# A convolution, SoLU and projection kernel: tiles in threes instead of pairs, with PSUM as three pairs of banks and two single ones

## The chip, the cores and the metric

One core of a Trainium2 chip. The metric is the device time of one launch in microseconds. Before the change it was 1185.45 us, the median of three runs (1185.33 to 1186.61).

The engines are called PE (matmuls; PEld is its loading of weights), DVE, ACT (ScalarE), POOL and SP (which here only issues DMAs).

## The reference

Two stages, of which the second takes the first's output as its rows:

```python
# conv: x is 8 x 4160 x 192, weight 8 x 7; causal, softmax over the 7 taps, one filter for each group of 24 columns
out = np.einsum('hk,bskhg->bshg', w, x_unf)
# mlp: 33280 rows of 192, w_in 192 x 1024, w_out 1024 x 192
h = x @ w_in
e = np.exp(h - np.max(h, axis=-1, keepdims=True))
solu = h * (e / (np.sum(e, axis=-1, keepdims=True) + 1e-09))
mu = np.mean(solu, axis=-1, keepdims=True)
var = np.mean((solu - mu) ** 2, axis=-1, keepdims=True)
out = ((solu - mu) / np.sqrt(var + 1e-06) * g_ln) @ w_out
```

## The kernel before, in words

The 33280 rows are 260 tiles of 128. They come out of 17 chunks of the sequence: two short ones at the start of the first batch, then fifteen of 2080 rows (half a batch, some 16 tiles). Everything is written out by hand, in the order in which each engine runs it; nothing is reordered afterwards.

Nearly all matmuls (the first three chunks' convolutions run in float32) work on float16 halves: a float32 value is kept as an upper float16 and the remainder as a lower one, and a product is the sum of three.

**Convolution of a chunk.** x is loaded (L150), its largest magnitude is taken on DVE (`sum_squares`, L171, eight of them for a chunk) and a scale worked out, then it is split into two halves on POOL (L226, L230, L233). Eight groups of matmuls with a band matrix (L271) make the convolution; each group lies in one PSUM bank, from which ACT takes the upper half (`upper`, L303) and DVE the lower one (`lower`, L312). DMA transposes (`turn`, L342) bring the result into `yT`, where the 192 columns, in halves, are three blocks of 128 partitions: two full upper/lower blocks, and one that holds the last 64 columns' upper half on 64 partitions and the lower half on the other 64. `double` (L355) copies 64 rows of `yT` to the other 64 partitions, as `y2`.

**A tile.** The first product (`emit_rows`, L727) is eight matmuls of 128 x 512 into a pair of banks, `ph`. What is left is the product of the last 64 columns with the lower half of the weights, which has only 64 rows: the *thirds* (`emit_third`, L752), two matmuls for a tile. Of one tile of a pair they run on the upper 64 rows of the array (from `yT`), of the other on the lower 64 (from `y2`), side by side. From `ph`:

- DVE scales it and takes the row's minimum (`emit_max`, L773), since the sign is turned;
- ACT takes the exponential and its sum into `e` (`emit_exp`, L780);
- DVE multiplies the two into `e` and sums (`numerators`, L790); with that `ph` is free;
- ACT casts the product to float16, `p` (L798), and sums its squares (L802);
- POOL makes the remainder (`emit_lo`, L807), and a DMA transpose on SP's queue (L809) turns both halves into `pT`;
- PE makes the second product from `pT`, 16 matmuls into one bank, `po` (`emit_out`, L824), five tiles later;
- DVE adds the two halves of `po` (`emit_evac`, L831), and every eight tiles POOL works out the factors of the rows (L878 to L888), which are applied on POOL or DVE (L893, L897) and stored (L906).

**PSUM** has eight banks: `ps_h` two pairs for `ph`, `ps_c` two single ones for convolutions and sums, `ps_o` two for `po`.

**The order.** The first six tiles have functions of their own (`first_two`, `second_two`, `third_two`), in which the weights are scaled too; from tile 6 on `two_steps` takes two tiles at a time. On PE: the first tile's eight matmuls, the four thirds of both tiles, the second tile's eight, then second products of two earlier tiles and up to two groups of the convolution of a later chunk. `chores` says by fractions of a chunk which group, turn, load and maximum falls to which tile. `tail` finishes the last five tiles; their second products have four banks, since `po` of every other one is put in `ps_c`.

## Time and profile before

| | |
|---|---|
| median of three runs | 1185.45 us |
| the profiled execution | 1186.39 us |
| its span, first to last instruction | 1184.6 us |
| mean granted clock of PE | 0.992 |
| PE busy | 1148.0 us (97%) |
| DVE busy | 1036.0 us (87%) |
| POOL busy | 961.1 us (81%) |
| ACT busy | 952.7 us (80%) |
| DMA queue q1, share of 16 engines | 97.9% |

The profile is of one execution, 0.9 us over the median. The clock is 1.00 almost throughout; two stretches of some 7 us, from 29.3 and 73.6 us, have 0.50 and 0.51. In a row of the timeline the first number is the start, the second how long the instruction or group lasted; "x4" is a group of four, and the brackets at the end tell how long the engine had been idle and what it waited for. Matmuls overlap by their pipeline, so what one costs is read from the start of one to the start of the next.

### The profile page before, as it was taken

The numbers are of one execution on the slowest core, as the hardware profiler recorded it, in microseconds if no ns is written. First come the engines' busy times: TensorE is split into PE (matmuls) and PEld (weight loads), VectorE is DVE, ScalarE is ACT, GpSimd is POOL, SyncE is SP. The second block draws the span as 40 slices with busy tenths as digits, with TensorE's granted clock in tenths as the row PEclk, the third lists the DMA queues.
The fourth block names the chain that finished last, engine by engine and source line by source line (L and its number), as shares of the span: only waits on it lengthen the run. The fifth ranks groups of instructions, "written<-read, shape, count | busy, mean of one in ns | idle before, by whom it ended". The sixth has DMA issues, their size and how long they took to land.

```text
span 1184.6 us, 22276 instructions
## 1 busy us (share of the span) xinstructions
PE 1148.0 (97%) x7678; PEld 676.9 (57%) x7678; DVE 1036.0 (87%) x2081; ACT 952.7 (80%) x1525; POOL 961.1 (81%) x951
## 2 busy tenths in 40 slices
PE   5989999999999999999999999999999999999997
PEld 3455555556565565656555565655655555565555
DVE  7889899998988989899899988999898898787785
ACT  6968888788888787888877788887878878888883
POOL 1726989998979699797978979898897979867675
PEclk9889999999999999999999999999999999999999
DMA  8789799999999999999999999999999998989986
GB/s 234 151 173 179 158 220 198 203 198 204 204 194 205 194 205 185 214 203 201 203 174 197 188 215 214 187 204 175 215 196 198 208 193 156 171 171 179 191 152 155
DMA packets 727295, 226.95 MB, mean 192 GB/s; under 512 B 651518, under 2 KB 725774, under 8 KB 727182
## 3 DMA queue, kind: packets, MB, share of 16 engines
q1 hardware_dynamic: 727182, 225.53, 97.9%
q8 instruction: 60, 0.98, 0.3%
q14 instruction: 53, 0.43, 0.1%
HBM read 33.00 MB, written 25.56 MB: 49 GB/s over the span
## 4 chain that ended last, share of the span: by engine, by line
PE 63%; POOL 13%; issue 8%; DVE 7%; ACT 4%; DMA 1%; POOLq 0%; ACTq 0%; DVEq 0%
PE po L824 28%; PE ph L727 26%; POOL p L807 8%; PE pc L271 4%; PE ph L752 4%; DVE e L790 2%; DVE ph L773 2%; ACT e L780 1%; ACT p L798 1%; DMA pT<-p 1%; POOL raw L893 1%; POOL t L887 1%; DVE cvm L337 1%; DVE xa L171 1%; POOL xs L226 1%
## 5 line engine op out<-in xcount | busy, mean ns | idle before, releaser
L807 POOL TENSOR_TENSOR p<-e,p 128x1024 f16<-128x1024 f32 x259 | 551.2, 2138 | 153.5 <-ACT p L798 153.3
L824 PE MATMUL po<-ohl,pT 128*128 128x384 f16 (+1 forms) x4200 | 548.6, 285 | 3.2 <-DVE raw L831 2.6
L824 PEld LDWEIGHTS <-pT 128*128 128x128 f16 x4200 | 382.0, 98 | 152.4 <-issue 4.3
L727 PE MATMUL ph<-whi,yT 128*128 128x512 f16 x1548 | 422.8, 382 | 15.2 <-DVE e L790 15.1
L780 ACT ACTIVATE e<-ph,sm 128x1024 f32<-128x1024 f32 x260 | 289.7, 1114 | 160.6 <-DVE ph L773 145.2
L773 DVE TENSOR_SCALAR_CACHE_REDUCE ph<-ph,cv 128x1024 f32<-128x1024 f32 x248 | 317.8, 1290 | 99.3 <-PE ph L752 56.6
L727 PEld LDWEIGHTS <-yT 128*128 128x128 f16 x2064 | 189.5, 98 | 265.9 <-issue 58.4
L790 DVE SCALAR_TENSOR_TENSOR e<-ph,cv,e 128x1024 f32<-128x1024 f32 x248 | 317.0, 1278 | 8.4 <-ACT e L780 5.6
L798 ACT CAST p<-e 128x1024 f16<-128x1024 f32 x260 | 270.6, 1041 | 38.5 <-DVE e L790 33.0
L802 ACT ACTIVATE sq<-e 128x1024 f32<-128x1024 f32 x260 | 274.5, 1056 | 4.0
L727 PE MATMUL ph<-wlo,yT 128*128 128x512 f16 x516 | 154.7, 382 | 0.0
L831 DVE TENSOR_REDUCE raw<-po 128x192 f32<-128x384 f32 x255 | 140.7, 552 | 0.0
L233 POOL TENSOR_TENSOR xs<-xr,xs 128x960 f16<-128x960 f32 (+1 forms) x56 | 107.7, 1924 | 2.3
L752 PE MATMUL ph<-wlo,yT 64*128 64x512 f16 x268 | 81.5, 384 | 0.0
L312 DVE SCALAR_TENSOR_TENSOR y<-pc,y 112x432 f16<-112x432 f32 (+5 forms) x140 | 72.4, 534 | 5.4 <-ACT y L303 5.2
L752 PE MATMUL ph<-wlo,y 64*128 64x512 f16 x252 | 76.3, 383 | 0.0
L271 PE MATMUL pc<-xs,taps_hi 128*112 128x240 f16 (+1 forms) x448 | 73.0, 261 | 0.3 <-ACT taps_hi L569 0.3
L171 DVE TENSOR_REDUCE xa<-xr 128x1 f32<-128x384 f32 x120 | 69.3, 618 | 0.0
L303 ACT ACTIVATE y<-pc 112x432 f16<-112x432 f32 (+5 forms) x140 | 63.1, 472 | 0.1
L230 POOL TENSOR_SCALAR xr<-xr,s 128x960 f32<-128x960 f32 (+1 forms) x56 | 57.7, 1030 | 2.4
L271 PE MATMUL pc<-xs,taps_lo 128*112 128x240 f16 (+1 forms) x224 | 58.5, 261 | 0.0
L887 POOL TENSOR_TENSOR t<-t,mhalf 128x8 f32<-128x8 f32 (+2 forms) x33 | 53.7, 1626 | 2.6
(146 smaller groups left out, 772.4 us busy)
## 6 DMA issues: line engine op xcount, KB each, us to landing
out_dram<-raw SPq DMA_DIRECT2D x127, 192.0 KB, 2.6
xr<-in_x_dram SPq DMA_DIRECT2D x41, 480.0 KB, 4.6
xr<-in_x_dram SPq DMA_DIRECT2D x22, 384.0 KB, 4.2
pT<-p SPq DMA_TRANSPOSE x260, 4.6
y<-yT SPq DMA_DIRECT2D x15, 140.0 KB, 2.5
y<-yT SPq DMA_DIRECT2D x15, 126.0 KB, 2.4
yT<-y SPq DMA_TRANSPOSE x102, 3.6
raw_out<-in_moe_w_out_dram SPq DMA_DIRECT2D x1, 1536.0 KB
```

The costliest lines, as they stand in the source:

```text
L233: (2.1 * size + 0.2, lambda: pool.tensor_tensor(xl, r, h, ALU.subtract)),
L271: nc.tensor.matmul(o, tp[:, h + j, :], r, start=q == 0, stop=q == len(ops) - 1)
L727: nc.tensor.matmul(bank, lhs, w[:, r, n * 512 : (n + 1) * 512], start=start and j == 0, stop=stop and j == len(ops) - 1,)
L752: nc.tensor.matmul(banks_of(t)[n], y[q, t.off : t.off + P], wlo[q, 1, n * 512 : (n + 1) * 512], start=start, stop=not start,)
L773: dve.tensor_scalar(t.ph, t.ph, t.cv[:, 0:1], None, ALU.mult, ALU.min, accum_out=t.bias)
L780: act.activation(t.e, t.ph, AF.Exp, bias=t.bias, scale=-1.0, accum_out=grp.z[:, g : g + 1])
L790: dve.scalar_tensor_tensor(t.e, t.ph, t.cv[:, 3:4], t.e, ALU.mult, ALU.mult, accum_out=t.grp.s1[:, t.g : t.g + 1],)
L798: act.copy(t.p16[:, :, 0, :], t.halves)
L802: act.activation(junk, t.e, AF.Square, accum_out=t.grp.s2[:, t.g : t.g + 1])
L807: eng.tensor_tensor(t.p16[:, :, 1, :], t.halves, t.p16[:, :, 0, :], ALU.subtract)
L824: nc.tensor.matmul(t.po[:, 0:n], t.pT[:, a, :], w, start=j == 0, stop=j == len(ops) - 1)
L831: dve.tensor_reduce(t.grp.raw[:, t.g, :], t.po[:, 0 : 2 * D].rearrange("p (a d) -> p d a", a=2), AX.X, ALU.add,)
```

## The change

PSUM is one pool of three pairs of banks (`pair(0)` to `pair(2)`) and two single banks that take turns (`single`): `po`, convolutions, sums of a column and small products all draw from these two, in the order of the program. From tile 8 on, `three_steps` takes three tiles a, b, c with the pairs 0, 1, 2. `emit_a` makes a's eight matmuls and then the thirds of all three in one place: a's beside b's, two at a time, then c's own two side by side, the first on the upper rows from `yT`, the second on the lower rows from `y2`. b's eight matmuls follow. The second products of three earlier tiles stand ahead of a's matmuls, between b's and c's, and after c's. Convolution groups stand at up to four places: after the first second product, after b's matmuls, after the second, and after the last second product.

The tiles 0 to 7 keep their pairs (`fourth_two` is new); the convolutions of chunk 1 are held there in the third pair (`hold`), and the thirds of both tiles, all on the upper rows, stand in two places as before. The maxima and loads of a triple (`others`) are written at its head, ahead of L831 of the first second product. The sum of squares of c is taken in the next triple. The load of `g_ln` moves from the end of the first loads to behind the first transposes and a load of chunk 1. In `tail`, the second products use the two single banks, and the factor of the first of the five tiles is worked out there, not three tiles earlier.

PE at the thirds of tiles 56 and 57 (`ph_56`, `ph_57` are the tiles' pairs of banks, `yT_4` and `y2_4` chunk 4's convolution), before:

```order
L727 MATMUL ph_56_3293<-whi_111,yT_4_2330 128x512
L752 LDWEIGHTS yT_4_2330
L752 MATMUL ph_56_3293<-wlo_112,yT_4_2330 128x512
L752 LDWEIGHTS y2_4_2331
L752 MATMUL ph_57_3302<-wlo_112,y2_4_2331 128x512
...
L727 LDWEIGHTS yT_4_2330
L727 MATMUL ph_57_3302<-whi_111,yT_4_2330 128x512
```

and with the change, with tile 58 as the third:

```order
L733 MATMUL ph_56_3311<-whi_104,yT_4_2317 128x512
L758 LDWEIGHTS yT_4_2317
L758 MATMUL ph_56_3311<-wlo_105,yT_4_2317 128x512
L758 LDWEIGHTS y2_4_2318
L758 MATMUL ph_57_3320<-wlo_105,y2_4_2318 128x512
...
L758 MATMUL ph_58_3321<-wlo_105,yT_4_2317 128x512
L758 LDWEIGHTS y2_4_2318
L758 MATMUL ph_58_3321<-wlo_105,y2_4_2318 128x512
L733 LDWEIGHTS yT_4_2317
L733 MATMUL ph_57_3320<-whi_104,yT_4_2317 128x512
```

What is left out repeats the four rows for the other bank. Six thirds stand in one place, where four stood; over the whole program the places fall from 134 to 92.

DVE over the same tiles (`sm` is a row's minimum, `po` a second product, `y16` the lower half of a convolution, `raw` the output), before:

```order
L773 TENSOR_SCALAR ph_56_3293,sm_56_3358<-ph_56_3293,cv_4_1443 128x1024
L773 TENSOR_SCALAR ph_57_3302,sm_57_3362<-ph_57_3302,cv_4_1443 128x1024
L790 SCALAR_TENSOR_TENSOR e_56_3360,s1_56_3289<-ph_56_3293,cv_4_1443,e_56_3360 128x1024
L831 TENSOR_REDUCE raw_48_3166<-po_51_3317 128x192
L790 SCALAR_TENSOR_TENSOR e_57_3364,s1_56_3289<-ph_57_3302,cv_4_1443,e_57_3364 128x1024
L312 SCALAR_TENSOR_TENSOR y16_5_10_3277<-pc_5_10_2_3334,y16_5_10_3277 112x9x48
L897 TENSOR_SCALAR raw_40_2744,t1_40_2445<-raw_40_2744,t2_40_2446 128x192
L831 TENSOR_REDUCE raw_48_3166<-po_52_3341 128x192
```

and with the change:

```order
L845 TENSOR_REDUCE raw_48_3173<-po_51_3287 128x192
L322 SCALAR_TENSOR_TENSOR y16_5_10_3219<-pc_5_10_2_3304,y16_5_10_3219 112x9x48
L911 TENSOR_SCALAR raw_32_2307,t1_32_1995<-raw_32_2307,t2_32_1996 128x192
L788 TENSOR_SCALAR ph_56_3311,sm_56_3343<-ph_56_3311,cv_4_1328 128x1024
L788 TENSOR_SCALAR ph_57_3320,sm_57_3347<-ph_57_3320,cv_4_1328 128x1024
L805 SCALAR_TENSOR_TENSOR e_56_3345,s1_56_3276<-ph_56_3311,cv_4_1328,e_56_3345 128x1024
L845 TENSOR_REDUCE raw_48_3173<-po_52_3358 128x192
L805 SCALAR_TENSOR_TENSOR e_57_3349,s1_56_3276<-ph_57_3320,cv_4_1328,e_57_3349 128x1024
L788 TENSOR_SCALAR ph_58_3321,sm_58_3410<-ph_58_3321,cv_4_1328 128x1024
L845 TENSOR_REDUCE raw_48_3173<-po_53_3393 128x192
L805 SCALAR_TENSOR_TENSOR e_58_3412,s1_56_3276<-ph_58_3321,cv_4_1328,e_58_3412 128x1024
```

The first two tiles of a triple stand as a pair did, minimum, minimum, product, evacuation, product. The third follows by itself: minimum, evacuation, product, with nothing else between them.

The diff, cut to its core:

```diff
-    ps_h = ctx.enter_context(tc.tile_pool(name="ps_h", bufs=2, space=PSUM))
-    ps_c = ctx.enter_context(tc.tile_pool(name="ps_c", bufs=2, space=PSUM))
-    ps_o = ctx.enter_context(tc.tile_pool(name="ps_o", bufs=2, space=PSUM))
+    ps = ctx.enter_context(tc.tile_pool(name="ps", bufs=1, space=PSUM))
...
+    def pair(slot, name):
+        return ps.tile([P, F], F32, name=name, tag=f"pair{slot}")
+    singles = 0
+    def single(name):
+        nonlocal singles
+        singles += 1
+        return ps.tile([P, 512], F32, name=name, tag=f"single{singles % 2}")
...
+    def emit_a(a, b, c):
+        a.ph = pair(0, f"ph_{a.i}")
+        emit_rows(a, True, False)
+        b.ph, c.ph = pair(1, f"ph_{b.i}"), pair(2, f"ph_{c.i}")
+        for t, n, low in (
+            (a, 0, False), (b, 0, True), (a, 1, False), (b, 1, True),
+            (c, 0, False), (c, 1, True),
+        ):
+            emit_third(t, n, low, t is not a)
...
     def emit_out(t):
-        ps, tag = (ps_c, "cv") if t.last and t.i % 2 else (ps_o, "po")
-        t.po = ps.tile([P, 512], F32, name=f"po_{t.i}", tag=tag)
+        t.po = single(f"po_{t.i}")
...
+    def three_steps(i):
+        a, b, c = ts = [prepare(i + j) for j in range(3)]
+        done = [tiles[j] for j in range(i - DEPTH + (i == PAIRED), i - DEPTH + 3)]
+        final = i == NT - 3
+        work = others(i, ts)
...
+        emit_out(done[0])
+        place(0)
...
+        if not final:
+            emit_a(a, b, c)
+        emit_rows(b, False, True)
+        emit_evac(done[0])
+        place(1)
+        uppers(0)
+        lowers(0)
...
+        emit_max(a)
+        emit_exp(a)
+        uppers(1)
+        emit_max(b)
+        lowers(1)
+        emit_exp(b)
+        numerators(a)
+        emit_lo(a, pool)
...
+        for d in done[1:2]:
+            emit_out(d)
+        place(2)
+        for d in done[1:2]:
+            emit_evac(d)
+        run_chain(4)
+        queue.run(3.8 if i < 20 else 2.0)
+        uppers(2)
+        emit_square(a)
+        numerators(b)
+        emit_lo(b, pool)
+        lowers(2)
+        if not final:
+            emit_rows(c, False, True)
+        for d in done[2:]:
+            emit_out(d)
+        place(3)
+        emit_max(c)
+        emit_exp(c)
+        emit_square(b)
+        run_chain(4)
+        for d in done[2:]:
+            emit_evac(d)
+        uppers(3)
+        lowers(3)
+        numerators(c)
+        queue.run(3.8 if i < 20 else 2.0)
+        emit_lo(c, dve if final else pool)
+        squares.append(c)
+        run_rows(i)
...
-    for i in range(6, NT, 2):
-        two_steps(i)
+    fourth_two(6)
+    for i in range(PAIRED, NT, 3):
+        three_steps(i)
     tail()
```

More of the change, by code (lines that the diff above doesn't have):

```diff
@@ L83, in total @@
         if bank is None:
-            bank = ps_c.tile([P, 512], F32, name=f"pt_{name}", tag="cv")
+            bank = single(f"pt_{name}")
         nc.tensor.matmul(
@@ L251, in product @@
             if bank is None:
-                bank = ps_c.tile([P, 512], F32, name=f"pc_{self.ch}_{a}_{h}", tag="cv")
+                bank = single(f"pc_{self.ch}_{a}_{h}")
             pc = bank[0:CW, 0 : (z - a) * n * HD].rearrange(
@@ L559, in split_taps @@
     def split_taps(q):
-        t = ps_c.tile([P, 512], F32, name=f"tph_{q}", tag="cv")
+        t = single(f"tph_{q}")
         for j in range(2):
@@ L939 @@
         pos += n
-    for t in tiles[-DEPTH:]:
-        t.last = True
     def chores(ch, k, n):
@@ L1080, in conv @@
                 queue.finish((c.ch, j))
-        return c.product(*hg), hg
+        return c.product(*hg, bank=bank), hg
     PAIRED = FIRST // P
-    assert spans[0][2] == PAIRED * P and PAIRED == 8 and NT % 2 == 0
-    for t in tiles:
-        t.split = False
-    early = []
+    assert spans[0][2] == PAIRED * P and PAIRED == 8 and (NT - PAIRED) % 3 == 0
+    early, doubles, squares = [], [], []
     def prepare(i):
@@ L1205, in third_two, with fourth_two @@
                 sum_up(c, h, i + 1)
[L1207 removed]
+    def fourth_two(i):
         t, u = prepare(i), prepare(i + 1)
[L1211 to L1232 removed]
+        done = [tiles[2], tiles[3]]
+        emit_two(t, u, lambda: None)
+        for d, j in zip(done, (2, 3)):
+            emit_out(d)
+            hold(chunks[1], j)
         emit_max(t)
@@ L1241, in two_steps @@
         emit_evac(done[0])
-        if first and not first[0][0].scaled:
-            run_chain(20)
-        for c, pc, hg in first:
+        for c, pc, hg in early[:1]:
             c.upper(pc, *hg)
         numerators(u)
-        for c, pc, hg in first:
+        for c, pc, hg in early[:1]:
             c.lower(pc, *hg)
+        emit_evac(done[1])
+        emit_lo(u, pool)
+        for c, pc, hg in early[1:]:
+            c.upper(pc, *hg)
+            c.lower(pc, *hg)
+        for blk in (1, 0, 2):
+            c.turn(blk, PW, c.nw)
@@ L1285, in tail @@
         assert all(t.grp.n == 1 for t in last)
-        for t in (a, b):
-            emit_out(t)
+        for t in squares:
+            emit_square(t)
+        emit_out(a)
+        emit_out(b)
+        ready(a)
+        emit_finish(a)
         queue.run(100.0)
-        emit_finish(a)
         ready(b)
```

188 lines of the change are left out of this document (97 added, 91 removed).

## The prediction

> **What bounds the kernel now.** I read the page first, then busy time by stretches, then the timeline of one quiet pair of tiles, then the waits.
>
> ```profile
> PE 1148.0 (97%) x7678; PEld 676.9 (57%) x7678; DVE 1036.0 (87%) x2081; ACT 952.7 (80%) x1525; POOL 961.1 (81%) x951
> PE 63%; POOL 13%; issue 8%; DVE 7%; ACT 4%; DMA 1%; POOLq 0%; ACTq 0%; DVEq 0%
> ```
>
> PE is busy 97% and holds 63% of the chain that ended last; POOL's 13% are stretches in which the chain could as well have been followed through PE. The stretches tell two stages apart (columns: us, then busy us of PE, PEld, DVE, ACT, POOL, then the granted clock, DMA share and GB/s):
>
> ```profile
> 60.00:90.00 30.00, 25.56 (x155) 14.53 (x152) 24.27 (x50) 20.88 (x35) 9.56 (x7) 0.89 0.80 174
> 90.00:120.00 30.00, 28.55 (x195) 16.93 (x194) 28.02 (x61) 25.86 (x41) 19.58 (x22) 1.00 0.93 183
> 120.00:150.00 30.00, 29.09 (x192) 16.28 (x192) 25.58 (x53) 26.13 (x47) 28.71 (x27) 1.00 0.80 162
> 250.00:1000.00 750.00, 748.37 (x5050) 440.27 (x5048) 672.73 (x1342) 613.16 (x976) 654.17 (x640) 1.00 1.03 197
> ```
>
> From 250 to 1000 us PE leaves 1.6 of 750 us free. There the matmuls themselves are the bound, and only fewer or cheaper ones help. From 60 to 150 us PE is idle 6.8 of 90 us, and loses 3.3 more in the first 30 us to a clock of 0.89. A quiet pair of tiles on PE:
>
> ```profile
> 387.12 4.08 PE L824 MATMUL po<-ohl,pT 128*128 128x384 f16 x32
> ...
> 391.04 0.59 PE L727 MATMUL ph<-whi,yT 128*128 128x512 f16 x2
> ...
> 391.90 1.03 PE L727 MATMUL ph<-whi,yT 128*128 128x512 f16 x4
> 392.86 0.39 PE L752 MATMUL ph<-wlo,yT 64*128 64x512 f16 x1
> 392.86 0.39 PE L752 MATMUL ph<-wlo,y 64*128 64x512 f16 x1
> 393.08 0.38 PE L752 MATMUL ph<-wlo,yT 64*128 64x512 f16 x1
> 393.09 0.38 PE L752 MATMUL ph<-wlo,y 64*128 64x512 f16 x1
> 393.40 0.60 PE L727 MATMUL ph<-whi,yT 128*128 128x512 f16 x2
> ...
> 394.27 1.03 PE L727 MATMUL ph<-whi,yT 128*128 128x512 f16 x4
> 395.13 4.08 PE L824 MATMUL po<-ohl,pT 128*128 128x384 f16 x32
> ```
>
> A pair takes 395.13 - 387.12 = 8.01 us. The same block of four L727 matmuls lasts 0.86 us ahead of second products (394.27 to 395.13) but 0.96 ahead of the thirds (391.90 to 392.86). The first two thirds, side by side, take 0.22 (392.86 to 393.08), the last two 0.32 (393.08 to 393.40). So each place of thirds costs 0.10 us on the way in and 0.10 on the way out, beside its work.
>
> **The change part by part.** *Fewer places.* The places of thirds now, one wait of the weight load each:
>
> ```profile
> PEld L752 <- issue: 57.6, 134, 0.8
> ```
>
> Eight of the 134 are in the first eight tiles and stay; 126 pairs become 84 triples, so 42 go: 42 x 0.20 = 8.4 us off PE. All matmul counts and shapes stay, and the six thirds of a triple still run in three slots, so a quiet triple takes 1.5 x 8.01 - 0.10 = 11.92 us. The Trainium skill (TensorE: Matmul & The Clock Gate, Step-by-step: what each phase is for) gives a drain of about 128 array cycles, and its page TensorEngine Tiling (Array Packing), Key Properties, says that changing the tiling mode drains the array. Two drains are 0.11 us by that, an estimate, which would make this term 4.5 us. The rows show nearly twice that, and the measurement decides.
>
> *The cover on DVE.* PE can keep its saving only if the others follow. DVE's load in the steady stage comes to this:
>
> ```profile
> L773 DVE TENSOR_SCALAR_CACHE_REDUCE ph<-ph,cv 128x1024 f32<-128x1024 f32 x166 | 213.5, 1291 | 67.1 <-PE ph L752 34.8 <-PE ph L727 31.0
> L773 DVE TENSOR_SCALAR_CACHE_REDUCE ph<-ph,cvm 128x1024 f32<-128x1024 f32 x8 | 10.1, 1266 | 2.0 <-PE ph L727 1.8 <-PE ph L752 0.2
> L171 DVE TENSOR_REDUCE xa<-xr 128x1 f32<-128x384 f32 x82 | 47.6, 617 | 0.0
> ```
>
> These are 174 tiles in 750 us: 12.93 us for three, convolutions included, of which DVE is busy 672.73 / 58 = 11.60. After the change PE needs 12.83, so DVE has 1.23 us to spare per triple. Today its free time is nearly all waiting for PE (69 of 77 us), which is slack. The new order spends it. Two tiles' minima used to follow each other, so that ScalarE's exponential of the first ran under the second's minimum. The third tile has no partner: its minimum (L773), one L831, then its product (L790) stand in a row. The times from one to the next:
>
> ```profile
> 387.32 1.29 DVE L773 TENSOR_SCALAR_CACHE_REDUCE ph<-ph,cv 128x1024 f32<-128x1024 f32 x1 [0.49 <-PE ph L727]
> 388.53 1.28 DVE L790 SCALAR_TENSOR_TENSOR e<-ph,cv,e 128x1024 f32<-128x1024 f32 x1
> 389.73 0.55 DVE L831 TENSOR_REDUCE raw<-po 128x192 f32<-128x384 f32 x1
> 390.20 1.27 DVE L790 SCALAR_TENSOR_TENSOR e<-ph,cv,e 128x1024 f32<-128x1024 f32 x1
> ```
>
> ```profile
> 142.34 1.27 DVE ph L773 x2
> 143.70 1.21 ACT e L780 x2
> 144.94 1.24 DVE e L790
> ```
>
> From a minimum's start to its product's start are 144.94 - 142.34 = 2.60 us at least; the minimum fills 1.21 of them and L831 0.47, so DVE stands still for 0.92. That leaves 0.31 of the 1.23 us. Two smaller waits can take that too: 2.60 - 2 x 1.21 = 0.18 between the first two tiles, and, in triples that have a convolution but no L171 at their head, the wait of L312 for the third tile's cast and the convolution's upper part on ScalarE:
>
> ```profile
> L798 ACT CAST p<-e 128x1024 f16<-128x1024 f32 x260 | 270.6, 1041 | 38.5 <-DVE e L790 33.0
> L303 ACT ACTIVATE y<-pc 112x432 f16<-112x432 f32 (+5 forms) x140 | 63.1, 472 | 0.1
> ```
>
> That is 1.04 + 0.47 less the 0.47 of an L831, about 1.0. So DVE's own time per triple is between 12.5 (no small wait, 11.60 + 0.92) and 13.5 (half the triples with the wait of 1.0, and 0.18 everywhere, plus what uneven triples lose), against PE's 12.83. PE waits for DVE where the third tile's pair must be free at the next thirds: from the end of its first products there are two second products (3.92) and the next tile's rows (1.82), 5.7 us, and the chain takes 2.60 + 1.20 = 3.8, a little more with the signals between engines. A lag under some 1.7 us costs nothing. Triples with three L171 at the head (3 x 0.62 = 1.9 us) stand beside triples with none, so some lag is carried and won back. In the steady stage, some 77 triples (from 170 to 1158 us at 12.83), I put the price between 0 and 0.7 x 77 = 54 us and take 4, near the low end: 12.5 holds only what stands in every triple, and is under PE's 12.83.
>
> ScalarE (613 of 750 us) and POOL (654) have no new step in the loop. POOL's remainder of a tile (L807) and its transpose are due a triple later:
>
> ```profile
> pT<-p SPq DMA_TRANSPOSE x260, 4.6
> ```
>
> On SP's queue the first tile's transpose now waits for a second product of its own triple (four buffers of pT), with the copies of y and the stores behind it; that product ends before POOL has the tile's remainder ready, so the wait adds nothing: 0, at most the 2 us of one second product once in a while.
>
> *The two single banks.* Second products, convolutions and sums shared four banks and now share two. In a triple with two convolutions the next user of a bank comes 2 us or more after the matmuls that it waits out, and the evacuations (0.47 for L831) stand ahead of the long DVE steps in the order; I take 0, and the case in which they are late is the same lag as above.
>
> *The start.* The longest PE wait from 60 us on, and what followed it:
>
> ```profile
> 74.43 0.61 PE L727 MATMUL ph<-whi,yT 128*128 128x512 f16 x1 [2.59 <-DVE e L790]
> 73.60:80.50 6.90, 6.07 (x16) 1.75 (x17) 3.79 (x13) 2.68 (x5) 2.51 (x3) 0.51 0.72 144
> ```
>
> Tile 10 waited 2.59 us for a pair of banks, and the clock then fell to 0.51 for 6.9 us. With a third pair, tile 10's rows wait for nothing of tile 8, and a second product and a convolution stand ahead of tile 8. The 6.8 us of idle PE and 3.3 us of clock could go. But DVE is busy 77.9 of these 90 us and gets the same forced 0.92 us in each of some six triples. Between -8 and +4; I take -2. The load of g_ln moves behind the first transposes on SP's queue, ahead of four loads of x; it has to land before ScalarE's L676:
>
> ```profile
> gl<-in_moe_g_ln_dram SPq DMA_DIRECT2D x1, 4.0 KB, 11.9
> 30.59 2.88 ACT L676 ACTIVATE e_out<-e_out,gl 128x192 f32<-128x192 f32 x8 [0.25 <-POOL gate L1121]
> ```
>
> Its 11.9 us were behind the large loads of the start; issued near 22 us it may come in time or some 3 us late. I take 0, up to +2.
>
> *The end.* There:
>
> ```profile
> 1158.29 4.08 PE L824 MATMUL po<-ohl,pT 128*128 128x384 f16 x32
> 1165.00 13.90 PE L824 MATMUL po<-ohl,pT 128*128 128x384 f16 x136 [2.63 <-DVE raw L831]
> ```
>
> PE waits 2.63 us for a bank; in the new order this evacuation comes earlier, but the five last tiles have two banks in place of four, and each needs the finish of the one two ahead. -1, from -4 to +4.
>
> **The sum.** -8.4 + 4 - 2 - 1 = -7.4 us. The profiled execution took 1186.39 us, its span of 1184.6 and 1.8 around it; it lies 0.9 over the median of 1185.45. From the median: 1178.
>
> **Rivals.** *DVE becomes the bound* (slower). Each third tile's minimum, exponential and product in a row, with the smaller waits, make DVE's triple longer than PE's 12.83 us, and PE stands at the thirds until L790 of the last third tile is done. For it: only 0.31 us per triple is left over. Against it: the allowance of 1.7 us, and lighter triples. At 0.4 us a triple it costs 31 us: 1185.45 - 8.4 - 3 + 31 = 1205. It decides from 0.15 us a triple (11.4 / 77). The Trainium skill (TensorEngine Tiling (Array Packing), PSUM Bottleneck) warns that packing the array doesn't speed up the evacuation of PSUM; it would show just so. *A draw*: at about that 0.15, the saving and the lag cancel: 1185. *The start is freed whole*: 6.8 and 3.3 us go there: 1185.45 - 8.4 - 10 = 1167. *The thirds don't pair*: the two of the third tile, which share one tile's bank pair, run one after the other; 84 x 0.22 = 18 us more: 1196. Against: they go to different banks and different row halves, as the pairs at 392.86 do.
>
> **How the numbers follow.** Forecast 0.52 (own range 1171 to 1183), freed start 0.10, draw 0.10, DVE the bound 0.25, no pairing 0.03. The range 1167 to 1205 leaves out half of the DVE case and some of the freed start. Over 0.2% (2.4 us, about what a measurement of this kernel can tell from no change) faster: 0.60; slower: 0.28; within: 0.12.
>
> **What would show it.** Right: 92 waits of the third's weight load; a quiet triple of 11.92 us; idle DVE ahead of the third tile's L790 near 0.9 us, and PE's waits for that line a few us in all after 200 us. Wrong: PE waiting at the thirds in most triples (DVE the bound), or two thirds of one tile 0.22 us apart.

## The result and the profile after

The changed kernel takes 1346.31 us (median of 4, 1344.46 to 1347.09), the kernel before 1186.03 us on the same chip: a ratio of 1.135 (95% interval 1.133 to 1.137). The forecast was 1178, with a range up to 1205. The change costs 160 us, and it does so nearly everywhere. The page of the changed kernel first:

```profile
PE 1179.1 (88%) x7678; PEld 697.0 (52%) x7678; DVE 1044.6 (78%) x2077; ACT 936.8 (70%) x1525; POOL 962.5 (72%) x953
PE 28%; POOL 25%; issue 17%; DVE 13%; ACT 8%; DMA 5%; SPq 3%; DVEq 0%; POOLq 0%; ACTq 0%
```

The same number of matmuls is there, and no engine is the bound any more: PE is busy 88% of the span, DVE 78%, POOL 72%, ScalarE 70%. Whoever reads only shares sees four engines with time to spare and a longer kernel; the difference is waits. The stretches shown for the kernel before, now of the changed kernel (us, busy us of PE, PEld, DVE, ACT, POOL, then the granted clock, DMA share, GB/s):

```profile
60.00:90.00 30.00, 20.69 (x138) 13.06 (x136) 22.66 (x47) 15.09 (x27) 6.35 (x6) 0.94 0.74 139
90.00:120.00 30.00, 23.85 (x154) 14.24 (x152) 19.86 (x40) 18.45 (x33) 14.80 (x16) 0.94 0.90 159
120.00:150.00 30.00, 27.86 (x186) 15.81 (x185) 25.03 (x52) 24.84 (x41) 22.09 (x17) 1.00 0.53 113
250.00:1000.00 750.00, 676.86 (x4434) 399.21 (x4434) 600.08 (x1171) 527.17 (x853) 567.36 (x545) 0.96 0.89 172
```

From 250 to 1000 us PE now stands idle 73.1 of 750 us (1.6 before), and the granted clock is 0.96. In the start (60 to 150 us) it is idle 17.6 us (6.8 before). Since a stretch of equal time holds different work, the table goes by tiles: the time from the first L733 (L727) of one tile to that of another, read from the timeline. The last column is what the profiled execution has in each stage more than the kernel before.

| stage | before | after | more |
|---|---|---|---|
| to tile 2 | 31.8 | 31.7 | -0.1 |
| tiles 2 to 26 | 123.7 | 144.9 | 21.2 |
| tiles 26 to 50 | 106.4 | 136.1 | 29.7 |
| tiles 50 to 242 | 828.9 | 925.9 | 97.0 |
| tile 242 to the end | 93.8 | 106.3 | 12.5 |
| span | 1184.6 | 1344.9 | 160.3 |

The largest loss, that of tiles 50 to 242, lies in stalls of several us. What DVE waited for in the changed kernel (us, times, longest):

```profile
DVE e L805 <- ACT e L795: 63.1, 77, 1.7
DVE raw L845 <- issue: 50.4, 11, 8.8
DVE raw L845 <- DMA out_dram<-raw: 33.4, 8, 8.8
```

The wait of L805 is the one foreseen (77 waits in 84 triples, 0.82 us each on the mean). The waits of L845 were not foreseen: in the kernel before this line waited for nothing (idle 0.0). L845 adds a second product into raw, the buffer that holds eight tiles' sums until their rows are scaled (L907, L911) and stored (L920). There are three such buffers. One group of eight, from its last L845 to the first L845 that needs its buffer again, in the changed kernel (rows of the timeline: start us, us, engine, line):

```profile
631.83 0.55 DVE L845 TENSOR_REDUCE raw<-po 128x192 f32<-128x384 f32 x1
...
714.69 1.01 SPq L920 DMA_DIRECT2D out_dram<-raw  x2
...
719.04 0.56 DVE L845 TENSOR_REDUCE raw<-po 128x192 f32<-128x384 f32 x1 [5.18 <-issue]
...
719.65 0.56 PE L281 MATMUL pc<-xs,taps_hi 128*112 128x240 f16 x2 [4.61 <-DVE raw L845]
```

And the same group in the kernel before:

```profile
553.09 0.56 DVE L831 TENSOR_REDUCE raw<-po 128x192 f32<-128x384 f32 x1
...
597.54 1.08 SPq L906 DMA_DIRECT2D out_dram<-raw  x1
...
624.03 0.55 DVE L831 TENSOR_REDUCE raw<-po 128x192 f32<-128x384 f32 x1
```

Before, the last store went out 44 us after the group's last L831, and the buffer was asked for 26 us later. After, the last store goes out 83 us behind (the first of the two in the row at 714.69), and the L845 that needs the buffer, which DVE had reached 5.18 us earlier, starts 4.3 us after it. The 23 groups from tile 32 to tile 215 are alike: the last store goes out 44 to 50 us behind the last L831 before and 69 to 90 us behind the last L845 after, and the next use of the buffer follows 22 to 27 us behind that store before, 2 to 9 us after. "Issue" means that the profile names no releaser for this one; for eight others it names the store, as the row above shows (33.4 us). With DVE stands PE, since the evacuation that waits is also what frees a single bank (L281 waits 4.61 us for L845). The clock then drops: 719 to 723 us is granted 0.57 on the mean, the next 4 us 1.00.

```profile
719.00:723.00 4.00, 3.35 (x13) 1.97 (x13) 3.12 (x8) 2.17 (x4) 1.05 (x1) 0.57 1.21 209
723.00:727.00 4.00, 4.00 (x26) 1.83 (x25) 2.37 (x4) 1.64 (x4) 3.38 (x9) 1.00 0.62 120
```

Why the stores come late stands in the code. Rows are scaled by `run_rows`, which is called twice in a step of the loop and takes one row a call, two when more than four wait. Neither these calls nor the number of rows a call was edited; but a step was two tiles and is three. Eight rows take six calls (two, two, then one each). Eight tiles used to bring eight calls and now bring 5.3, so the next group comes before the last one is through. The stores, too, are issued once a step (`run_stores`).

Where PE bounds the triple, it is as short as forecast. A quiet triple on PE, with no convolution and no stall:

```profile
689.66 0.59 PE L733 MATMUL ph<-whi,yT 128*128 128x512 f16 x2
...
691.92 0.38 PE L758 MATMUL ph<-wlo,yT 64*128 64x512 f16 x1
691.92 0.38 PE L758 MATMUL ph<-wlo,y 64*128 64x512 f16 x1
...
697.66 4.08 PE L838 MATMUL po<-ohl,pT 128*128 128x384 f16 x32
701.58 0.37 PE L281 MATMUL pc<-xs,taps_hi 128*112 128x240 f16 x2
```

701.58 - 689.66 = 11.92 us, the forecast to the digit; the third tile's two thirds start together.

### The profile page after: what moved, and what is told of

Read it like the earlier page. It is cut to its first block, busy times and chain, and to the rows that moved or that the text cites. A ratio compares the mean times of both kernels' runs of the same rounds, so it can differ in the third digit from the quotient of the medians.

```text
span 1344.9 us, 22210 instructions
## 1 busy us (share of the span) xinstructions
PE 1179.1 (88%) x7678; PEld 697.0 (52%) x7678; DVE 1044.6 (78%) x2077; ACT 936.8 (70%) x1525; POOL 962.5 (72%) x953
## 4 chain that ended last, share of the span: by engine, by line
PE 28%; POOL 25%; issue 17%; DVE 13%; ACT 8%; DMA 5%; SPq 3%; DVEq 0%; POOLq 0%; ACTq 0%
POOL p L822 14%; PE po L838 13%; PE ph L733 12%; DVE e L805 4%; DVE ph L788 3%; DMA out_dram<-raw 3%; ACT e L795 3%; ACT p L813 2%; POOL xs L243 2%; PE ph L758 2%; POOL xr L240 2%; DMA pT<-p 2%; PE pc L281 2%; POOL xs L236 2%; POOL raw L907 2%
## 5 line engine op out<-in xcount | busy, mean ns | idle before, releaser
L822 POOL TENSOR_TENSOR p<-e,p 128x1024 f16<-128x1024 f32 x259 | 551.6, 2136 | 297.1 <-ACT p L813 296.6
L838 PE MATMUL po<-ohl,pT 128*128 128x384 f16 (+1 forms) x4200 | 557.7, 290 | 85.7 <-DVE raw L845 54.7
L838 PEld LDWEIGHTS <-pT 128*128 128x128 f16 x4200 | 388.1, 100 | 264.9 <-issue 105.4
L795 ACT ACTIVATE e<-ph,sm 128x1024 f32<-128x1024 f32 x260 | 289.5, 1114 | 237.1 <-DVE ph L788 190.5
L733 PE MATMUL ph<-whi,yT 128*128 128x512 f16 x1548 | 428.9, 387 | 6.6 <-DVE e L805 6.3
L805 DVE SCALAR_TENSOR_TENSOR e<-ph,cv,e 128x1024 f32<-128x1024 f32 x248 | 317.5, 1280 | 66.7 <-ACT e L795 59.4
L788 DVE TENSOR_SCALAR_CACHE_REDUCE ph<-ph,cv 128x1024 f32<-128x1024 f32 x248 | 314.4, 1286 | 25.4 <-PE ph L758 13.9
L733 PEld LDWEIGHTS <-yT 128*128 128x128 f16 x2064 | 196.7, 100 | 239.0 <-issue 49.5
L817 ACT ACTIVATE sq<-e 128x1024 f32<-128x1024 f32 x260 | 273.2, 1051 | 0.0
L845 DVE TENSOR_REDUCE raw<-po 128x192 f32<-128x384 f32 x255 | 140.7, 552 | 105.9 <-issue 50.4
L733 PE MATMUL ph<-wlo,yT 128*128 128x512 f16 x516 | 157.4, 387 | 0.0
L281 PE MATMUL pc<-xs,taps_hi 128*112 128x240 f16 (+1 forms) x448 | 75.2, 266 | 45.2 <-DVE raw L845 22.6
L322 DVE SCALAR_TENSOR_TENSOR y<-pc,y 112x432 f16<-112x432 f32 (+5 forms) x140 | 72.1, 531 | 48.5 <-ACT y L313 48.5
L758 PE MATMUL ph<-wlo,yT 64*128 64x512 f16 x268 | 75.6, 387 | 2.9 <-DVE e L805 2.9
L181 DVE TENSOR_REDUCE xa<-xr 128x1 f32<-128x384 f32 x120 | 67.9, 615 | 3.4 <-DMA xr<-in_x_dram 3.3
L758 PE MATMUL ph<-wlo,y 64*128 64x512 f16 x252 | 70.4, 385 | 0.0
L281 PEld LDWEIGHTS <-taps_hi 128*112 128x112 f16 x448 | 50.4, 132 | 33.0 <-issue 18.7
L281 PE MATMUL pc<-xs,taps_lo 128*112 128x240 f16 (+1 forms) x224 | 59.6, 266 | 0.0
```

The costliest lines, as they stand in the source:

```text
L281: nc.tensor.matmul(o, tp[:, h + j, :], r, start=q == 0, stop=q == len(ops) - 1)
L733: nc.tensor.matmul(bank, lhs, w[:, r, n * 512 : (n + 1) * 512], start=start and j == 0, stop=stop and j == len(ops) - 1,)
L758: nc.tensor.matmul(banks_of(t)[n], y[q, t.off : t.off + P], wlo[q, 1, n * 512 : (n + 1) * 512], start=start, stop=not start,)
L788: dve.tensor_scalar(t.ph, t.ph, t.cv[:, 0:1], None, ALU.mult, ALU.min, accum_out=t.bias)
L795: act.activation(t.e, t.ph, AF.Exp, bias=t.bias, scale=-1.0, accum_out=grp.z[:, g : g + 1])
L805: dve.scalar_tensor_tensor(t.e, t.ph, t.cv[:, 3:4], t.e, ALU.mult, ALU.mult, accum_out=t.grp.s1[:, t.g : t.g + 1],)
```

## The experiments

The stages of all profiled kernels, by the same tiles (us), and the median of each. "+ list in order" is added to "more rows", each later "+" to the row above it; "tail" is "+ tail in the pairs". The kernel before was measured again beside each, at 1184.75 to 1186.23 us.

| kernel | 2 to 26 | 26 to 50 | 50 to 242 | 242 to end | median |
|---|---|---|---|---|---|
| before | 123.7 | 106.4 | 828.9 | 93.8 | 1186.0 |
| before, one call of `run_rows` a pair | 123.4 | 112.9 | 881.2 | 94.0 | 1245.3 |
| after | 144.9 | 136.1 | 925.9 | 106.3 | 1346.3 |
| more rows | 144.3 | 130.5 | 850.2 | 102.4 | 1259.2 |
| four buffers of raw | 142.4 | 129.3 | 847.7 | 103.1 | 1256.3 |
| more rows, sums late | 154.8 | 135.8 | 872.7 | 102.4 | 1297.1 |
| more rows, own place for c | 143.0 | 131.6 | 853.6 | 102.4 | 1263.3 |
| + list in order | 144.9 | 107.2 | 850.8 | 102.8 | 1240.0 |
| + third tile's gap | 142.6 | 105.7 | 846.8 | 102.9 | 1231.9 |
| + tail in the pairs | 142.7 | 105.7 | 841.9 | 101.3 | 1227.5 |
| + convolutions moved | 143.6 | 106.2 | 842.1 | 101.4 | 1227.3 |
| tail, rows on POOL | 143.4 | 106.2 | 838.6 | 101.3 | 1222.4 |
| tail, rows on ScalarE | 145.8 | 105.5 | 841.2 | 101.4 | 1223.7 |
| + early transposes | 139.8 | 105.0 | 841.3 | 101.4 | 1220.8 |

The theory after the result: late rows hold the buffers of raw. The rival: the third tile's minimum, exponential and product make DVE the bound, and L845 is only where DVE happens to stand. (Where an expectation speaks of idle PE in a stage, it is the sum, from matmul start to matmul start in the trace, of what a gap has over the time of the matmul itself, gaps over 0.35 us alone.)

**More rows per call.**

```
-        for _ in range(4 if late else 2 if len(rows) > 4 else 1):
+        for _ in range(4 if late else 3 if len(rows) > 4 else 2):
```

> The changed kernel with one more row scaled per call of run_rows (3 in place of 2, 2 in place of 1). Theory (late rows): the loop calls run_rows twice per step, and a step is now three tiles, so the last store of a group of eight goes out 82 us after the group's last L845 (47 in the kernel before), and the first L845 of the third group after it waits for that buffer: 91 us of DVE in all, 82 us of idle PE and 17 us of lower clock in the steady stage. With more rows per call the delay falls under 60 us, the idle time of L845 under 5 us, and the time to about 1346 - 82 - 17 = 1247, from 1235 to 1260. Rival (the third tile's minimum, exponential and product in a row make DVE the bound, my rival of the prediction): the wait only moves, to L805 or L788, PE still waits for L805 in the steady stage, and the time stays over 1300.

Measured: 1259.17 us (ratio 1.062, 1.060 to 1.065), 87 us less than the changed kernel. The theory's 1247 was 12 too low, just inside its range. The last store now goes out 50 to 69 us behind (the same 23 groups), not under 60 in all of them, and no L845 waits for its buffer any more.

**Four buffers of raw**, with rows and stores as late as they were (the scratch tile of the squares becomes float16 to make room; ScalarE's L817 takes 1.05 us either way):

```
...
-            self.raw = self.mk("raw", [P, GMAX, D], 3)
+            self.raw = self.mk("raw", [P, GMAX, D], 4)
```

> The changed kernel with four buffers of raw in place of three (room for it comes from float16 junk for the squares); rows and stores stay as late as they are. Theory (late rows matter only through the buffer): the buffer is needed a group later, some 33 us, so the idle time of L845 goes although the last store still comes 75 to 85 us behind, and the time is within 10 us of the kernel with more rows, about 1247. Rival (the rows themselves, in bursts on DVE and POOL, delay the tiles): L845 waits no more, but the time stays over 1290. DVE-bound rival: over 1300 in both.

Measured: 1256.32 us (1.061, 1.059 to 1.063). The page's group of L845 (last figures: idle us before it), in the changed kernel, with more rows, and with four buffers:

```profile
L845 DVE TENSOR_REDUCE raw<-po 128x192 f32<-128x384 f32 x255 | 140.7, 552 | 105.9 <-issue 50.4
```

```profile
L845 DVE TENSOR_REDUCE raw<-po 128x192 f32<-128x384 f32 x255 | 140.5, 551 | 8.0 <-PE po L838 7.9
```

```profile
L845 DVE TENSOR_REDUCE raw<-po 128x192 f32<-128x384 f32 x255 | 140.5, 551 | 8.5 <-PE po L838 8.2
```

Either edit takes the wait away, one by earlier rows, the other by a buffer that is needed later while the last store still comes 64 to 84 us behind. Late rows as such cost nothing; they cost through the buffer. The rival falls for this part: had DVE's order been the bound, the wait would have moved.

**The kernel before with one call of run_rows a pair**, between tiles 16 and 228. The reverse test, in the other program:

```
         run_chain(4)
-        run_rows(i, False)
+        if i < 16 or i >= NT - 32:
+            run_rows(i, False)
```

> The kernel before with one call of run_rows per pair of tiles in place of two, between tiles 16 and 228. Theory (late rows): 8 rows in 4 calls need a backlog of over 4, so the last store comes some 20 us later, 65 to 72 us behind the last L831; the 24 us of slack at reuse shrink to 0 to 6 us, and the time is 1185 to 1200. Rival (rows have no part in it): the delay may grow, but the time is 1185 whatever the slack.

Measured: 1245.28 us in its one run, 60 over the kernel before. The direction is the theory's, the size not: I had the delay at 65 to 72 us and the time at 1200 at most; the delay came to 74 to 81, so that the slack was not shrunk but used up. Its page and its timeline:

```profile
L831 DVE TENSOR_REDUCE raw<-po 128x192 f32<-128x384 f32 x255 | 140.4, 551 | 103.4 <-DMA out_dram<-raw 55.2
```

```profile
323.02 0.53 SPq L906 DMA_DIRECT2D out_dram<-raw  x1
...
325.70 0.56 DVE L831 TENSOR_REDUCE raw<-po 128x192 f32<-128x384 f32 x1 [4.71 <-DMA out_dram<-raw]
```

The store goes out at 323.02 and DVE goes on 2.7 us later. Here the profile names the store as the releaser. A kernel with pairs, untouched otherwise, gets the stalls of the changed one (103.4 us idle, 105.9 there).

**Sums late.** A second loss is one single wait, at 257 us in the changed kernel, from its waits of PE:

```profile
PE pc L281 <- POOL xs L243: 21.4, 1, 21.4
```

The first theory was that the sums of a chunk (L181), which the change puts at the head of a step, make the following chunk's work come too early. The test, on the kernel with more rows, put them back to the end:

```
         run_rows(i)
+        sums_of(work, ts)
         for k in work.get("open", []):
```

(`sums_of` is the loop of `sum_up` that stood in `others`, called at a step's head.)

> The kernel with more rows per call, and the sums of the chunk two or three ahead (L181, L217) put back to the end of a step, where the kernel before has them. Theory (early sums): in the changed kernel the steps that split chunk 5 are queued ahead of the rest of chunk 4's, so that a convolution of chunk 4 forces ten POOL operations at once at 235 to 259 us, PE waits 21.8 us; with sums later chunk 4's rest is done first and 15 to 22 us go against the kernel with more rows alone. Rival (POOL is behind for another reason, since each tile's remainder takes it 2.1 us): the wait stays within 5 us.

Measured: 1297.05 us, 38 more than without it, and the wait stayed (21.3 us). The theory falls. The cost came from elsewhere:

```profile
PE pc L95 <- DVE xa L217: 41.8, 15, 4.2
PE pc L281 <- POOL xs L243: 21.3, 1, 21.3
```

PE runs ahead of DVE into the next triple, and its L95 then waits there 1 to 4 us, 15 times, for sums at the very end of DVE's step. So the head is a better place for them than the end.

**POOL's list in order.** POOL's order in the changed kernel ahead of that wait, with the chunk in the names:

```
138 L243 TENSOR_TENSOR xs_5_2151<-xr_5_1_1320,xs_5_2151 128x960
...
144 L243 TENSOR_TENSOR xs_5_2151<-xr_5_3_1673,xs_5_2151 128x768
145 L240 TENSOR_SCALAR xr_4_3_1002<-xr_4_3_1002,s_4_1327 128x768
146 L243 TENSOR_TENSOR xs_4_1653<-xr_4_3_1002,xs_4_1653 128x768
```

Chunk 5's steps stand ahead of chunk 4's last one, which PE needs first. They are put at the list's head when a chunk's scale is known, and whoever needs an item runs all that stand before it. In the kernel before, chunk 4 was done by then.

```
-            queue.items[0:0] = [
+            queue.items += [
```

> The changed kernel with more rows per call, and the steps that split a chunk's input put at the end of POOL's list of steps, not at its head. Theory (order of the list): chunk 5's steps were put ahead of the rest of chunk 4's, and the convolution that needs chunk 4 then forced all of them at once; PE stood still 21 us at 252 us. In the order of the chunks this wait falls under 5 us, and the time by 15 to 22 us against the kernel with more rows alone (1259): 1237 to 1244. Rival (POOL has too much work by then, whatever the order): the wait and the time stay within 5 us.

Measured: 1240.02 us, 19.2 less than with more rows alone, all of it in tiles 26 to 50 (130.5 to 107.2). The theory holds, the rival falls.

**The third tile's gap on DVE.** With these two mended, PE still idles in the stage from tile 50 to 242 (length less busy: 24.5 us; 1.6 of 828.9 before):

```profile
283.90:1134.70 850.80, 826.29 (x5580) 491.09 (x5579) 748.43 (x1462) 666.99 (x1080) 713.40 (x697) 1.00 0.99 190
```

```
+        uppers(3)
         emit_square(b)
         ...
-        uppers(3)
+        sums(2, i + 2)
+        numerators(c)
         lowers(3)
-        numerators(c)
```

> As the one before, and in the loop the sums (L181) no longer at the head of a step but up to two of them in the third tile's wait for its exponential, the convolution's upper part ahead of the square on ScalarE, and its lower part behind the third product on DVE. Theory (DVE's order: the forced 0.92 us of the third tile, the 0.8 us waits of L322, and three L181 ahead of the evacuation that frees a bank): of the 28.7 us that PE idles between tiles 50 and 242 (2.1 before) 10 to 20 go, and the time falls by as much. Rival (two single banks are too few in any order): PE goes on waiting for L845 and L322, and the time falls by under 5 us.

Measured: 1231.93 us, 8.1 less; the stage is 4.0 shorter, not 10 to 20 (in the kernel of the next test, whose loop is the same, it is 8.9 shorter). What DVE and PE waited for from 310 to 1110 us, with the list in order, and then with the gap filled:

```profile
PE po L838 <- DVE raw L845: 14.3, 15, 1.7
...
DVE e L805 <- ACT e L795: 51.7, 61, 0.9
DVE y L322 <- ACT y L313: 25.3, 26, 1.7
```

```profile
PE po L838 <- DVE raw L845: 7.6, 12, 1.1
PE po L838 <- DMA pT<-p: 6.9, 9, 1.8
...
DVE y L322 <- ACT y L313: 32.2, 40, 1.8
DVE e L805 <- ACT e L795: 22.1, 28, 0.9
```

DVE's forced wait for L795 was cut by 30 us, of which 7 came back at L322, and PE got 4 of them in this profile: its wait for L845 halved, and one for the transposes of p (L838 for pT) rose in its place, 3.1 to 6.9. Neither side is wholly right.

**The tail in the pairs.**

```
-        emit_out(c)
+        spare = [pair(j, f"po_{q.i}") for j, q in enumerate((c, d, e))]
+        emit_out(c, spare[0])
...
```

> As the one before, and the last three tiles' second products go to the pairs of banks, which are free by then, not to the two single ones. Theory (two banks for five last tiles): PE's wait of 6.4 us for L864 at the end goes, and the time falls by 4 to 7 us. Rival (the chain of the last tiles' remainders and transposes sets the end): under 2 us.

Measured: 1227.47 us, 4.5 less. That is within the theory's 4 to 7, but by luck: the end is only 1.6 us shorter (102.9 to 101.3), which is the rival's case. The wait of 6.4 us for L864 is gone, and these stand in its place:

```profile
PE po L838 <- DVE raw L845: 3.7, 2, 2.9
PE ph L733 <- DVE e L805: 3.4, 1, 3.4
PE po L838 <- DMA pT<-p: 3.4, 2, 2.3
```

The other 4.9 us of the profile are in tiles 50 to 242, where the program is the same; the cause of that is open. So up to 5 us between two such kernels, or in this stage of them, are not to be read closely, and what the gap alone gave there lies between 4 and 9 us.

**An own place for the third tile's thirds**, on the kernel with more rows:

```
-            (c, 0, False), (c, 1, True),
...
         emit_rows(b, False, True)
+        for n in range(NH):
+            emit_third(c, n, bool(n), True)
```

> The changed kernel with more rows per call, and the third tile's two thirds in a place of their own, behind the second tile's rows: 84 places more. Theory (PE still bounds most triples, and a place costs 0.10 us on the way in and 0.10 out): 84 x 0.20 = 17 us more than with more rows alone (1259), about 1276. Rival (DVE bounds the triples by now): the added time lies in PE's waits, and the time rises by under 6 us.

Measured: 1263.32 us, 4.2 more, the rival's case. The stage from tile 50 to 242 with more rows, and with the 64 added places in it:

```profile
305.40:1155.60 850.20, 826.00 (x5580) 491.17 (x5579) 747.35 (x1460) 665.97 (x1078) 711.88 (x697) 1.00 0.99 190
```

```profile
305.00:1158.60 853.60, 837.18 (x5580) 486.16 (x5579) 750.81 (x1460) 665.57 (x1079) 712.44 (x696) 1.00 0.98 189
```

The same matmuls keep PE busy 11.2 us longer (0.175 a place, near the 0.20 of the forecast), and PE idles 7.8 us less (24.2 to 16.4). So two thirds of what a place costs, or saves, is by now paid out of PE's waiting for others.

**Convolutions moved.** An edit that missed:

```
-            put(0.0, 0.375, "conv", [(c1, hg) for hg in c1.groups()[:4]])
+            put(0.18, 0.36, "conv", [(c1, hg) for hg in c1.groups()[:4]])
```

> As the last of the row before (more rows, POOL's list in order, sums in the gap, tail in the pairs), and the first four convolutions of chunk 2 moved from tiles 8 to 13 to tiles 11 to 13. Theory (a wait in order on ScalarE): the upper part of chunk 2's first convolution writes the y that chunk 1's transposes still read, ScalarE waits 10 us for them at 68 to 78 us with tile 8's exponentials queued behind, and DVE and PE follow; a step later the y is free, and 4 to 8 us of the start go (1227 to 1219..1223). Rival (two single banks for exact convolutions that take 1.0 us a head group on PE): with four of them in one step PE waits as long or longer for L322, and the time is within 2 us of 1227 or over it.

Measured: 1227.33 us, no change. Chunk 1 has eight tiles, so the four convolutions fall on tiles 9 and 10, still in the first triple; ScalarE's wait is as it was (9.9 us). It tells nothing about the theory.

**Rows on POOL, and rows on ScalarE**, both on the kernel with the tail in the pairs (two edits, cut to their core):

```
-                g.row(j, pool if j % 2 and i < NT else dve)
+                g.row(j, pool if (j % 2 or 26 <= i < NT - 18) and i < NT else dve)
```

```
+            if eng is act:
+                act.activation(o, o, AF.Copy, scale=u)
```

> As the last of the row before, with all rows of tiles 26 to 242 on POOL, none on DVE: some 100 x 0.33 us less for DVE and 100 x 0.43 more for POOL. Theory (DVE bounds many triples): of the 18.8 us that PE idles there 8 to 14 go, and the time falls from 1227 to about 1215. Rival (POOL and the transposes behind its remainders are as late): PE waits for pT instead (6.7 us now) and the time stays within 3 us or rises.

> As the kernel with the tail in the pairs, with all rows of tiles 26 to 242 on ScalarE: neither DVE (0.33 us a row) nor POOL (0.43) has them. Theory (DVE and POOL both bound the triples by now: rows on POOL took the waits for L845 from 7.0 to 2.4 us, but those for pT rose from 10.5 to 20.8): PE's idle time between tiles 50 and 242 falls from 15.9 (rows on POOL) to 6 to 11 us, the time from 1222 to 1212..1218. Rival (what is left comes from the two single banks and the uneven triples, not from load): within 3 us of 1222.

Measured: 1222.35 us on POOL, 1223.72 on ScalarE, 5.1 and 3.8 less than with rows on both DVE and POOL. The ratios to the kernel before are 1.0315 (1.0300 to 1.0331) and 1.0320 (1.0304 to 1.0336), that of the kernel they start from 1.0350 (1.0335 to 1.0366): a small gain for POOL, between its two forecasts, and none that is clear for ScalarE, whose stage from tile 50 to 242 is as long as it was (841.2, 841.9) and whose time is the rival's. PE's waits from 310 to 1110 us, on POOL, then on ScalarE with DVE's longest beside them:

```profile
PE po L838 <- DMA pT<-p: 7.1, 7, 2.7
...
PE po L838 <- DVE raw L845: 2.4, 6, 0.5
```

```profile
PE po L838 <- DVE raw L845: 7.6, 18, 0.9
...
DVE y L322 <- ACT y L313: 63.5, 45, 2.2
```

Rows on POOL take the waits for L845 and bring those for transposes; on ScalarE it is the other way round, though DVE and POOL then have 29 and 37 us less to do in the stage than in the kernel it starts from. Less load on these two alone shortens nothing here. But the test is not a clean one: ScalarE has 66 us more to do, and DVE's wait for it at L322 went from 33.5 to 63.5 us. That it matters when DVE's evacuation comes, and not how much DVE has to do, is argued, not shown.

**Early transposes.** In the start ScalarE waits once for 10 us: the upper part of chunk 2's first convolution writes where chunk 1's transposes still read, and tile 8's exponential is queued behind it. Chunk 1's transposes were put ahead of two tiles' own on SP's queue (both L822 with their transposes are emitted after the turns).

> As the one before, and in the fourth pair of tiles chunk 1's transposes are put on SP's queue ahead of the two tiles' own. The run that moved chunk 2's convolutions left them in the first triple (chunk 1 has 8 tiles), so ScalarE's wait of 10 us for these transposes was not touched by it. Theory (that wait costs the start): ScalarE's wait falls from 10 to 5 or 6 us, and the time by 2 to 5 us. Rival (the single banks' order sets the start): the wait falls, the time stays within 2 us.

Measured: 1220.81 us, 2.9 less than with rows on ScalarE alone (ratios 1.030, 1.027 to 1.033, and 1.032, 1.030 to 1.034: the intervals overlap, so the times alone do not show it). ScalarE's longest wait for that line from 60 to 170 us, before this edit and with it:

```profile
ACT y L313 <- DMA yT<-y: 10.2, 1, 10.2
```

```profile
ACT y L313 <- DVE s L112: 5.8, 1, 5.8
```

The wait falls by 4.4 us and is now one for the chunk's scale; tiles 2 to 26 take 139.8 in place of 145.8 (142.7 with the tail in the pairs, whose start is the same program as that of rows on ScalarE). That this wait costs a part of the start, 3 to 6 us, is what the profiles say; the times do not settle it.

## Why the prediction was wrong, point by point

*The step that failed: what is done at a rate per step, which the sum had at 0.* On POOL and SP the prediction said that ScalarE and POOL "have no new step in the loop", that POOL's work is "due a triple later", and of SP's queue, "with the copies of y and the stores behind it", that "the wait adds nothing: 0". I priced instructions that moved and not those whose rate is set by the step. The rows keep their line and their text, but two calls a step are two calls for three tiles. The delay from the last evacuation to the last store went from 44 to 83 us in the group shown; the kernel before had 26 us of slack there, which I had not looked up, so its loss became a wait for the buffer. Undone, it gives back 87 us (or 90, by the buffer) of 160, and the reverse edit costs the kernel before 60. No rival had it: all of mine were about DVE's, PE's and the thirds' own instructions.

*A second one of the same kind.* The order of POOL's list depends on when a chunk's scale is known against how far the list is worked off; shown by the list in order: 19 us. I had read POOL's remainder of a tile and its transpose, and not this list.

*The signs.* All that I had named for being right came true: 92 places (94 waits of the weight load for "issue", since some have two), a quiet triple of 11.92 us, 0.92 us of idle DVE, and some 6 us of waiting for L805 after 200 us in the changed kernel; neither sign of being wrong did. They tested the terms that I had priced, and most of the loss came from work that I had not priced.

*Fewer places (-8.4).* Right: 11.92 us a quiet triple, and 0.175 us for a place in the run that adds 64. It is not to be seen in the time, since PE is no longer the bound, and hardly in PE's busy time (827.3 us between tiles 50 and 242 before, 826.0 with more rows), in which a matmul ahead of a wait counts with its whole 0.38 us and not with the 0.21 to the next start. Two drains by the Trainium skill (TensorE: Matmul & The Clock Gate, Step-by-step: what each phase is for) would be 0.11 us, an estimate; the run has more, and the measurement decides.

*The cover on DVE (+4, bounds 0 and 54).* The mechanism was there: an idle 0.92 us before the third tile's product, as worked out.

```profile
514.51 1.28 DVE L805 SCALAR_TENSOR_TENSOR e<-ph,cv,e 128x1024 f32<-128x1024 f32 x1 [0.92 <-ACT e L795]
```

With the rows mended, the stage of 64 triples is 21.3 us longer than before (850.2 to 828.9) although its matmuls lost places: 0.33 us a triple and more, for this lag and the single banks together, within the bounds but far from the end I took. The place was wrong as well. I looked for PE waiting for L805; with more rows there are three such waits in all (8.6 us), at the start and at the end, none between tiles 50 and 242. PE waits for L845, since a single bank comes free late. The rule of the Trainium skill that the prediction weighed (TensorEngine Tiling (Array Packing), PSUM Bottleneck: packing the array does not make PSUM's evacuation faster) fits this, in the 14.3 us shown above.

*The two single banks (0).* Wrong, and it is where the lag shows. In the start PE's L838 and L281 wait for DVE's L845, L322 and L203, and in the quiet stage L838 waits 14.3 us for L845 until DVE's order is changed, then 7.6. I had reasoned from two us between a bank's users, which holds where DVE is on time.

*The start (-2, from -8 to +4).* Wrong by more than its range: tiles 2 to 26 take 21.2 us more. The idle PE there rose from 6.8 to 17.6 us, as the rows at the top show; the wait that I wanted gone (L727 for L790) did go, and five others of over 2 us came. From PE's waits between 60 and 170 us, the longest before and the longest after:

```profile
PE ph L727 <- DVE e L790: 7.5, 7, 2.6
```

```profile
PE pc L281 <- DVE y L322: 7.0, 4, 3.1
```

The early transposes took 3 to 6 us of it, by the profiles. The rest was not undone by any run.

*The end (-1, from -4 to +4).* Wrong: 12.5 us more, 8.6 with more rows. The bank that I spoke of (the finish of the tile two ahead) is 6.4 to 7.2 us of waiting; freeing it gave only 1.6, since L845, L805 and pT are next.

*What stays open.* The best of these kernels (1220.81) is still 35 us, 3%, behind the kernel before. By its stages 16 us of that are in the start, 12 between tiles 50 and 242, 8 at the end. Waits for single banks lie in all three in the profile, but outside the tail no run gave the kernel another bank, so that part is argued, not shown.

## What to carry to other kernels

When a loop's step grows, list everything that is done "so many times a step" (rows taken, stores flushed, items of a list) and work out its rate per tile before and after; then look up, for each buffer behind such work, the time from its last use to its reuse. That a buffer's writer waits for nothing today does not tell how near the wait is: the slack is read between the last store and the next write of the same buffer (26 us here, against a step's 4 us a tile). And when an engine has waits of several kinds, taking one away can mostly buy the next one: here 30 us less for L805 gave PE 4 to 9. And choose the signs of being right so that one of them looks at what the prediction has at 0; the signs here all came true and the time was 160 us off.

## What was not expected of the hardware

The granted clock fell to 0.57 after one PE wait of 4.61 us and was back at 1.00 within 4 us, so that this stall cost more than its length. Over the stage from tile 50 to 242 PE is busy 848.2 us for what takes 826.0 with more rows.

```profile
312.70:1238.60 925.90, 848.19 (x5580) 500.75 (x5579) 748.67 (x1462) 667.00 (x1080) 712.93 (x697) 0.97 0.90 175
```

Two tiny copies of DVE took some ten times as long while POOL worked on a wide tensor as with POOL idle (kernel with more rows):

```profile
477.43 2.02 POOL L243 TENSOR_TENSOR xs<-xr,xs 128x960 f16<-128x960 f32 x1
477.75 1.72 DVE L346 COPY cvm<-cv 128x4 f32<-128x4 f32 x1
...
479.39 2.13 POOL L822 TENSOR_TENSOR p<-e,p 128x1024 f16<-128x1024 f32 x1
...
479.51 2.04 DVE L347 COPY cvm<-cv 64x4 f32<-64x4 f32 x1
```

```profile
94.49 0.17 DVE L346 COPY cvm<-cv 128x4 f32<-128x4 f32 x1
```

Both copies end as POOL's instruction ends (479.47 and 479.45, 481.55 and 481.52). Earlier in the same kernel's start the first of them took 0.17, with POOL idle. The Trainium skill (SBUF — State Buffer, SBUF: two separate sides) says that a DVE instruction in a two-port mode and one of GpSimd hold one pair of ports in turn, for a whole instruction each. The trace agrees with it in the ends of the four rows; in which mode the copies run no row tells, and no run here took POOL's work away from them. Not every instruction of POOL holds them up: in the kernel before six of the same copies (L336, L337) ran in 0.16 us each inside POOL's L887 (128x8, 1.67 us).
